# Filling, joined pieces and a state product on four quadrants in a linear-attention and two-layer kernel

## The chip, the cores and the metric

The kernel runs on one core of a Trainium2 chip. The metric is the device time of one execution in microseconds; the time before is the median of three runs. The engines are TensorE (PE; its weight loads are shown apart as PEld), VectorE (DVE), ScalarE (ACT), GpSimd (POOL) and the sync engine (SP), whose queue issues all the transfers here.

## What is computed

A gated linear attention over 4 batches, 8 heads, 768 steps and 48 features a head, and two feed-forward layers on its output. All numbers are float32.

```python
for t in range(S):                       # S = 768
    state = alpha[:, :, t, :, None] * state + einsum('bhd,bhe->bhde', k[:, :, t], v[:, :, t])
    y[:, :, t] = einsum('bhd,bhde->bhe', q[:, :, t], state)
x = y.transpose(0, 2, 1, 3).reshape(B * S, H * D)      # 3072 x 384
h = x @ w_in                                           # 384 x 2048
x = where(h > 0, h, exp(minimum(h, 0)) - 1) @ w_out
g = x @ w_gate                                         # 384 x 1536
return (g * sigmoid(g) * (x @ w_val)) @ w_out2
```

## The kernel before

**Tiling.** The 768 steps are cut into 6 chunks of 128; a unit u is one chunk of one batch (24 units, chunk c = u // 4, batch b = u % 4). In a unit the 8 heads are 4 pairs: head 2p lies on partitions 0 to 47 and head 2p+1 on 64 to 111 (`PR` = 112), the pairs side by side. The first layer works on 4 units at once (512 columns), its 384 input features in 3 blocks of 128 partitions. The heads of pairs 0 to 2 fill 96 partitions of each block; those of pair 3 are cut in three and laid into the gaps (partitions 48 to 63 and 112 to 127) by transfers.

**One unit.** `A`, `N`, `M` make the decays and scale K and Q on VectorE, ScalarE and GpSimd (on VectorE alone for u < 4). `E` multiplies K and Q (`scores`) and masks them (`causal`) into the tile A; for c > 0 it first copies the batch's state `sc` into `sbd`, a block-diagonal tile, on ScalarE. `Dk` turns K (`flip`, four transposes) and copies it out (`keep`) into KT. `Gs` makes the outer product of KT and V (`outer`) and brings `sc` up to date (`state`, VectorE). `Hy` makes the output y: `values` is the product of `sbd` and Q (four matmuls of 112x112) and that of V and A (eight, on two column tiles). `high` rounds y into the layer's input x (pairs 0 to 2) and into x3 (pair 3) on ScalarE; the remainder is made by `low` on VectorE, and for u < 4 by `minus`, a matmul with the negative identity, and `rest` on ScalarE. `gaps` moves x3 into the gaps of x, six transfers a chunk.

**PSUM.** `bank` gives the one tile `aps` (for u < 4 in turn with `acc2`) to `flip`, `outer` and `values`; `pair` gives `ape`, two banks, to `scores`.

**The layers.** `moe1` and `moe2`: each product is three matmuls of rounded and remainder parts (`mm3`), so a group of a block of features is 9 matmuls of 128x128x512. `mm1` makes h, `mm2` the accumulation acc, two groups behind. Weights come packed as raw words and are unpacked by `weight` on ScalarE and VectorE from two raw buffers. `SEGMENTS` lists the order of the first layer: (chunk, first and last block, the attention chunk added before it): chunk 0 first half with attention chunk 1; chunk 1 first half; chunk 0 second half; chunk 1 second half with attention chunk 2; then chunks 2 to 5, each with the next attention chunk. The second layer follows.

**Order.** Nothing of this is issued as it is written. Every step is `plan.add`ed with its engine and a planned duration, and `Plan.run` lays out all of them as a list schedule: at each moment the ready step with the longest tail goes first; `soon` lifts a step's rank and `lag` adds a margin ahead of it. The engines' orders are then fixed by hand (`Pinned`, line 128 records every operation, so most rows have that line). Up to the first `mm1`, `run` calls `warm` ahead of each TensorE step with the planned idle time, and `warm` puts in matmuls on zeros (tile `idle`), one for each 0.22 us; `at.warm(6.8)` puts 30 ahead of all.

## Time and profile before

| | us |
|---|---|
| median of 3 runs (989.09 to 989.59) | 989.59 |
| the profiled execution | 990.69 |
| its span, first to last instruction | 988.9 |
| TensorE busy | 973.4 |
| VectorE busy | 541.0 |
| ScalarE busy | 512.7 |
| GpSimd busy | 69.3 |

All times in the rows below are microseconds from the span's start. In a timeline row stand the start, the stretch that the merged instructions cover, the engine, the line, the operation, the tile written and the tiles read, and the number of instructions; brackets give the idle time before them and what ended it. Matmuls overlap and their ends are modelled, so a matmul group is read from start to start. A float32 matmul has two records, one in the rounded format (the layers, the transposes, `minus`) has one.

### The profile page before, as it was taken

The numbers are of one execution on the slowest core, as the hardware profiler recorded it, in microseconds if no ns is written. First come the engines' busy times: TensorE is split into PE (matmuls) and PEld (weight loads), VectorE is DVE, ScalarE is ACT, GpSimd is POOL, SyncE is SP. The second block draws the span as 40 slices with busy tenths as digits, with TensorE's granted clock in tenths as the row PEclk, the third lists the DMA queues.
The fourth block names the chain that finished last, engine by engine and source line by source line (L and its number), as shares of the span: only waits on it lengthen the run. The fifth ranks groups of instructions, "written<-read, shape, count | busy, mean of one in ns | idle before, by whom it ended". The sixth has DMA issues, their size and how long they took to land.

```text
span 988.9 us, 13352 instructions
## 1 busy us (share of the span) xinstructions
PE 973.4 (98%) x5354; PEld 811.2 (82%) x5354; DVE 541.0 (55%) x840; ACT 512.7 (52%) x910; POOL 69.3 (7%) x51
## 2 busy tenths in 40 slices
PE   9899999999999999999999999999999999999997
PEld 4577788878887888888888888888888888888886
DVE  4999888667646653533677763334333334333332
ACT  3889999666776765555898542212212212212111
POOL 0122011123211310100000000000000000000000
PEclk9999999999999999999999999999999999999999
DMA  4646434333302301100434311001001001000001
GB/s 192 222 158 209 162 114 159 108 102 118 101 1 85 129 6 43 36 14 1 160 128 183 127 52 65 1 1 64 1 1 57 8 1 45 9 1 32 1 1 36
DMA packets 20662, 72.51 MB, mean 73 GB/s; under 512 B 2672, under 2 KB 5744, under 8 KB 17648
## 3 DMA queue, kind: packets, MB, share of 16 engines
q1 hardware_dynamic: 20592, 71.58, 21.2%
q8 instruction: 44, 0.72, 0.3%
q14 instruction: 26, 0.21, 0.1%
HBM read 58.20 MB, written 11.01 MB: 70 GB/s over the span
## 4 chain that ended last, share of the span: by engine, by line
PE 91%; ACT 3%; DVE 3%; DMA 2%; issue 0%; SPq 0%; ACTq 0%; DVEq 0%
PE gv L128 30%; PE acc L128 19%; PE h L128 18%; PE q L128 15%; PE aps L128 4%; PE idle L128 2%; PE ape L128 2%; DMA in<-qkva 1%; DVE in L128 1%; ACT raw L128 1%; DVE raw L128 1%; DMA raw<-w 1%; ACT e L128 1%; ACT R L128 1%; ACT x L128 0%
## 5 line engine op out<-in xcount | busy, mean ns | idle before, releaser
L128 PE MATMUL gv<-x,wt 128*128 128x512 f32 x1296 | 308.1, 391 | 0.0
L128 PEld LDWEIGHTS gv<-x,wt 128*128 128x128 f32 x1296 | 242.2, 188 | 48.0
L128 PE MATMUL h<-x,wt 128*128 128x512 f32 x864 | 215.6, 394 | 1.4 <-DMA x<-x 1.4
L128 DVE TENSOR_TENSOR s<-gv,s 128x512 f32<-128x512 f32 x144 | 99.6, 691 | 210.7 <-ACT s L128 167.3
L128 PE MATMUL acc<-g,wt 128*128 128x512 f32 x864 | 214.5, 393 | 0.2 <-DVE g L128 0.2
L128 PEld LDWEIGHTS h<-x,wt 128*128 128x128 f32 x864 | 159.7, 188 | 37.0 <-ACT r L128 1.7
L128 PEld LDWEIGHTS acc<-g,wt 128*128 128x128 f32 x864 | 160.4, 188 | 35.0 <-DVE g L128 0.6
L128 PE MATMUL q<-wt,u 128*128 128x384 f32 x864 | 163.0, 337 | 0.0
L128 PEld LDWEIGHTS q<-wt,u 128*128 128x128 f32 x864 | 153.6, 188 | 5.6
L128 ACT ACTIVATE s<-gv 128x512 f32<-128x512 f32 x72 | 43.1, 598 | 176.6 <-PE gv L128 176.6
L128 DVE SCALAR_TENSOR_TENSOR e<-e,r 128x512 f32<-128x512 f32 x96 | 68.6, 715 | 98.0 <-ACT r L128 97.9
L128 ACT ACTIVATE u<-s 128x512 fp32r<-128x512 f32 x72 | 45.4, 631 | 123.6 <-DVE s L128 123.2
L128 ACT ACTIVATE e<-h 128x512 f32<-128x512 f32 x96 | 57.1, 595 | 67.8 <-PE h L128 67.4
L128 DVE TENSOR_TENSOR g<-e,g 128x512 fp32r<-128x512 f32 x96 | 67.3, 701 | 29.8 <-ACT g L128 29.5
L128 ACT ACTIVATE g<-e 128x512 fp32r<-128x512 f32 x96 | 60.3, 628 | 28.9 <-DVE e L128 28.5
L128 DVE SCALAR_TENSOR_TENSOR raw<-raw 128x768 int32<-128x768 int32 x68 | 67.9, 1000 | 12.0 <-ACT raw L128 10.9
L128 DVE TENSOR_TENSOR u<-s,u 128x512 fp32r<-128x512 f32 x72 | 49.8, 692 | 40.6 <-ACT u L128 40.5
L128 ACT ACTIVATE e<-e 128x512 f32<-128x512 f32 x96 | 60.7, 632 | 2.9
L128 ACT ACTIVATE raw<-raw 128x768 f32<-128x768 f32 x68 | 58.9, 905 | 3.1 <-DMA raw<-w 2.9
L128 ACT ACTIVATE r<-h 128x512 f32<-128x512 f32 x96 | 55.9, 582 | 0.0
L128 POOL TENSOR_TENSOR in<-in 112x512 f32<-112x512 f32 x20 | 30.1, 1504 | 249.9 <-DVE in L128 130.7
L128 POOL TENSOR_TENSOR in<-in,R 112x512 f32<-112x512 f32 x20 | 37.0, 1849 | 79.5 <-ACT R L128 79.5
(78 smaller groups left out, 614.7 us busy)
## 6 DMA issues: line engine op xcount, KB each, us to landing
raw<-w SPq DMA_DIRECT2D x34, 768.0 KB, 4.2
in<-qkva SPq DMA_DIRECT2D x23, 1024.0 KB, 5.4
x2r<-x2d SPq DMA_DIRECT2D x18, 256.0 KB, 3.4
out<-y SPq DMA_DIRECT2D x24, 192.0 KB, 2.0
x2d<-o SPq DMA_DIRECT2D x12, 256.0 KB, 2.3
x<-x SPq DMA_DIRECT2D x36, 64.0 KB, 4.3
half<-o SPq DMA_DIRECT2D x6, 256.0 KB, 4.0
part<-half SPq DMA_DIRECT2D x6, 256.0 KB, 6.1
```

Of the source, the lines that this page charges most:

```text
L128: ins = getattr(self.engine, name)(*a, **k)
```

## The change

- Filling: the 30 matmuls ahead of all go; one filling matmul stands for 0.36 us of planned idle time in the first stretch and for 0.25 us in the later ones, in place of 0.22 us.
- Joined pieces: for u >= 4 `scores` and `flip` are one TensorE step, and so are `outer` and `values`. The output y then lies in the `ape` tile, across its two banks, and `aps` is left to `flip` and `outer`.
- The state's product reads `sc` directly, as eight 48x48 matmuls on the four 64x64 quadrants; `sbd` and its ScalarE copies go. `CROSS` says which pairs (2 and 3) have their two heads on changed sides of x, so that pair p and pair p + 2 use the four quadrants and different banks.
- Chunk 0 (`first`): a padded copy `vz` of V's heads 6 and 7, made on GpSimd, lets 12 matmuls of V and A write all 128 partitions of the three blocks; one `high`, one `minus` and one `rest` follow, and no `gaps`.
- The first layer's w_in tiles are loaded with the halves of block 2 swapped: three transfers in place of one for 8 of the 16 tiles. `gaps` of the other chunks reads x3 by the new sides.

```diff
+CROSS = (0, 0, 1, 1)
...
-                fill(start[i] - last)
+                fill(start[i] - last, last)
...
-            syn.dma_start(out=w.raw.rearrange("p a t -> p (a t)"), in_=src.bitcast(I32))
+            to, of, n = w.raw.rearrange("p a t -> p (a t)"), src.bitcast(I32), 2 * G * 128
+            if not cross:
+                syn.dma_start(out=to, in_=of)
+                return
+            m = n * CROSS.index(1)
+            syn.dma_start(out=to[:, 0:m], in_=of[:, 0:m])
+            for j in range(2):
+                syn.dma_start(
+                    out=to[64 * j:64 * j + 64, m:KD * n], in_=of[64 - 64 * j:128 - 64 * j, m:KD * n])
...
-        plan.add("SP", 0.5, load, w=[hk, lk], kb=768)
+        plan.add("SP", 1.5 if cross else 0.5, load, w=[hk, lk], kb=768)
...
-            for _ in range(int((us - 0.2) / 0.22)):
+            for _ in range(int((us - 0.2) / (0.25 if start else 0.36))):
...
-            if c:
-                def state():
-                    for j in range(2):
-                        r = slice(64 * j, 64 * j + D)
-                        act.activation(
-                            out=self.sbd[u % 2][r, :, 64 * j:64 * j + D], in_=self.sc[b][r], func=AF.Copy)
-                plan.add("ACT", 0.65, state, r=[("sc", b)], w=[("sbd", u % 2)])
...
+            turned = self.Dk(u) if u >= B else None
+            if turned:
+                key, flip, keep = turned
+                def both():
+                    scores()
+                    flip()
+                plan.add("PE", 1.65, both, r=[K, Q], w=[*keys, key], soon=SOON, lag=MARGIN)
+                plan.add("ACT", 0.48, keep, r=[key], w=["KT"])
...
+            def apart():
+                pool.tensor_copy(
+                    self.vz[:, :, :, D:64],
+                    d["v"][:, 2 * KD:H, 0:D].rearrange("p j (i e) -> p j i e", i=KD))
+            def values():
+                d["oy"] = o = bank()
+                for p in range(KD):
+                    for j in range(2):
+                        i = j ^ CROSS[p]
+                        ten.matmul(
+                            out=o[64 * j:64 * j + 64, p * C:(p + 1) * C], lhsT=d["v"][:, 2 * p + i, :],
+                            rhs=d["A"][:, i, p], start=p == 0, stop=False)
+                for p in range(KD):
+                    for j in range(2):
+                        i = j ^ CROSS[p]
+                        ten.matmul(
+                            out=o[64 * j:64 * j + 64, p * C:(p + 1) * C], lhsT=self.vz[:, i, p],
+                            rhs=d["A"][:, i, KD], start=False, stop=p == KD - 1)
+            def high():
+                if 0 not in xt:
+                    new_x(0)
+                act.activation(
+                    out=xt[0][:, 0, :, ts], in_=d["oy"][:, 0:KD * C].rearrange("p (a c) -> p a c", a=KD),
+                    func=AF.Copy)
+            def minus():
+                ten.matmul(
+                    out=d["oy"][:, 0:KD * C], lhsT=self.neg, rhs=xt[0][:, 0, :, ts],
+                    start=False, stop=True, skip_group_check=True)
...
+                o = self.pe.tile([128, 2, 512], F32, tag="ape", name="ape").rearrange("p a n -> p (a n)")
+                d["oy"] = o = o[:, 256:768]
                 cols = [slice(p * C, (p + 1) * C) for p in range(NP)]
                 for p, cs in enumerate(cols):
-                    if c:
+                    for j in range(2):
+                        i = j ^ CROSS[p]
                         ten.matmul(
-                            out=o[0:PR, cs], lhsT=self.sbd[u % 2][0:PR, p, 0:PR], rhs=d["Q"][0:PR, p],
-                            start=p == 0, stop=False,
+                            out=o[64 * j:64 * j + (D if j else 64), cs],
+                            lhsT=v[:, 2 * p + i, 0:D] if j else v[:, 2 * p + i, :],
+                            rhs=d["A"][:, i, p], start=p % 2 == 0, stop=False,
                         )
-                for p, cs in enumerate(cols):
-                    ten.matmul(
-                        out=o[0:64, cs], lhsT=v[:, 2 * p, :], rhs=d["A"][:, 0, p],
-                        start=not c and p == 0, stop=p == NP - 1,
-                    )
-                    ten.matmul(
-                        out=o[64:PR, cs], lhsT=v[:, 2 * p + 1, 0:D], rhs=d["A"][:, 1, p],
-                        start=not c and p == 0, stop=p == NP - 1,
-                    )
+                for p in range(2):
+                    for pp in (p, p + 2):
+                        for i in range(2):
+                            j = i ^ CROSS[pp]
+                            r = slice(64 * i, 64 * i + D)
+                            ten.matmul(
+                                out=o[64 * j:64 * j + D, cols[pp]], lhsT=self.sc[b][r, pp],
+                                rhs=d["Q"][r, pp], start=False, stop=p == 1,
...
+            renew = self.Gs(u)
+            if renew:
+                okey, outer, state = renew
+                def both():
+                    outer()
+                    values()
+                plan.add("PE", 2.2, both, r=["A", V, Q, "KT", ("sc", b)], w=[key, okey],
+                         soon=SOON, lag=MARGIN)
+                plan.add("DVE", 0.65, state, r=[okey, F], w=[("sc", b)])
...
-            if b == B - 1:
+            if b == B - 1 and c:
...
-        w1[g, s] = weight(plan, lambda: P.wp, "w", w1d[g, s], 2 * NG1)
+        w1[g, s] = weight(plan, lambda: P.wp, "w", w1d[g, s], 2 * NG1, not (plan.now or s))
...
-    at.warm(6.8)
```

## Rows read from the trace of the kernel before

**Rows 1.** From the page: TensorE in part 1, busy time, share, instructions.

```profile
PE 973.4 (98%) x5354; PEld 811.2 (82%) x5354; DVE 541.0 (55%) x840; ACT 512.7 (52%) x910; POOL 69.3 (7%) x51
```

**Rows 2.** The chain that ended last, 0 to 105 us: start, duration, what.

```profile
1.07 18.50 PE idle L128 x72
...
97.85 2.35 DMA x<-x
...
100.33 2.35 PE h L128 x9
```

**Rows 3.** Windows of the filling matmuls alone: stretch, length, busy (count), clock, DMA.

```profile
1.00:6.60 5.60, 5.53 (x14) 1.00 0.70 245
6.60:19.50 12.90, 12.90 (x60) 1.00 0.62 259
...
46.00:52.00 6.00, 4.92 (x22) 1.00 0.90 327
```

**Rows 4.** Timeline of all engines, 0 to 30 us.

```profile
9.85 0.69 DVE L128 SCALAR_TENSOR_TENSOR in<-N,in 112x512 f32<-112x512 f32 x1 [0.19 <-ACT N L128]
...
19.50 1.16 PE L128 MATMUL acc<-in 48*128 48x128 f32 x16
...
20.76 1.29 DVE L128 TENSOR_TENSOR A<-acc,mask 128x512 int32<-128x512 int32 x2 [7.80 <-PE acc L128]
```

**Rows 5.** Windows of all engines: stretch, length, busy time and count of each engine.

```profile
21.20:95.90 74.70, 69.61 (x606) 51.06 (x605) 72.60 (x123) 66.11 (x129) 14.57 (x10) 1.00 0.54 187
100.30:133.00 32.70, 32.67 (x156) 26.89 (x157) 26.26 (x38) 30.35 (x51) 1.61 (x2) 1.00 0.34 124
```

**Rows 6.** Timeline of all engines, 30 to 62 us.

```profile
47.69 0.64 ACT L128 ACTIVATE x<-acc 112x128 fp32r<-112x128 f32 x2
...
48.36 3.94 SPq L128 DMA_DIRECT2D x<-x  x6
...
54.01 4.37 PE L128 MATMUL h<-x,wt 128*128 128x512 f32 x18
```

**Rows 7.** Timeline of TensorE, 215 to 300 us.

```profile
220.30 1.13 PE L128 MATMUL aps<-in,sbd 112*112 112x128 f32 x8 [0.88 <-DVE T L128]
```

**Rows 8.** Timeline of TensorE, 292 to 345 us, units 16 to 19.

```profile
293.38 2.21 PE L128 MATMUL h<-x,wt 128*128 128x512 f32 x9
...
299.28 0.67 PE L128 MATMUL aps<-in,KT 128*64 128x48 f32 x16
299.88 2.33 PE L128 MATMUL h<-x,wt 128*128 128x512 f32 x9
302.05 1.04 PE L128 MATMUL aps<-in,sbd 112*112 112x128 f32 x8
303.02 1.09 PE L128 MATMUL aps<-A,in 128*64 128x128 f32 x16
304.03 2.35 PE L128 MATMUL acc<-g,wt 128*128 128x512 f32 x9
306.32 1.16 PE L128 MATMUL ape<-in 48*128 48x128 f32 x16
307.41 0.60 PE L128 MATMUL aps<-ident,in 112*128 112x112 f32 x4
307.78 2.29 PE L128 MATMUL h<-x,wt 128*128 128x512 f32 x9
310.00 0.67 PE L128 MATMUL aps<-in,KT 128*64 128x48 f32 x16
...
342.35 2.21 PE L128 MATMUL acc<-g,wt 128*128 128x512 f32 x9
344.39 0.84 PE L128 MATMUL h<-x,wt 128*128 128x512 f32 x3
```

**Rows 9.** Timeline of TensorE, 378 to 421 us, units 20 to 23.

```profile
379.07 2.20 PE L128 MATMUL acc<-g,wt 128*128 128x512 f32 x9
...
418.93 2.21 PE L128 MATMUL h<-x,wt 128*128 128x512 f32 x9
```

More of the change, by code (lines that the diff above doesn't have):

```diff
@@ L191, in __init__, with weight @@
             self.key = key
-    def weight(plan, pool, tag, src, slots):
+    def weight(plan, pool, tag, src, slots, cross=False):
         w = Box(*turn(tag, slots))
@@ L269, in __init__ @@
             self.sc = [cp.tile([128, NP, D], F32, name=f"sc{b}") for b in range(B)]
-            self.sbd = [cp.tile([128, NP, 128], F32, name=f"sbd{b}") for b in range(2)]
             self.ident = cp.tile([128, 128], F32, name="ident")
@@ L276, in __init__ @@
             self.neg = cp.tile([128, 128], F32R, name="neg")
+            self.vz = cp.tile([128, 2, KD, 64], F32, name="vz")
             self.x3 = cp.tile([128, 2, TB], F32R, name="x3")
@@ L298, in init @@
         def init(self):
+            self.z = self.cp.tile([128, 128], BF16, name="wz")
+            vec.memset(self.z, 0.0)
             vec.memset(self.zero, 0.0)
@@ L313, in init, with warm @@
             nc.gpsimd.tensor_copy(self.mask, t)
-            for t in self.sbd:
-                nc.gpsimd.memset(t, 0.0)
-        def warm(self, us):
+        def warm(self, us, start):
             if self.idle is None:
-                self.z = self.cp.tile([128, 128], BF16, name="wz")
-                vec.memset(self.z, 0.0)
                 self.idle = ph.tile([128, TB], F32, tag="h", name="idle")
-            for _ in range(int((us - 0.2) / 0.22)):
+            for _ in range(int((us - 0.2) / (0.25 if start else 0.36))):
                 ten.matmul(
@@ L471, in causal @@
                     )
-            plan.add("PE", 1.25, scores, r=[K, Q], w=keys, soon=SOON, lag=MARGIN)
+            turned = self.Dk(u) if u >= B else None
[5 more added lines that the diff above has]
+                plan.add("PE", 1.65, both, r=[K, Q], w=[*keys, key], soon=SOON, lag=MARGIN)
+                plan.add("ACT", 0.48, keep, r=[key], w=["KT"])
+            else:
+                plan.add("PE", 1.25, scores, r=[K, Q], w=keys, soon=SOON, lag=MARGIN)
             plan.add("DVE", 1.24 if len(keys) > 1 else 1.1, causal, r=keys, w=["A"])
@@ L503, in state, with first, rest @@
                 vec.tensor_tensor(out=sc[0:PR], in0=kv, in1=pc, op=ALU.mult)
+            if c:
+                return key, outer, state
             plan.add("PE", 0.75, outer, r=["KT", V], w=[key], soon=SOON, lag=MARGIN)
-            plan.add("DVE", 0.65 if c else 0.3, state, r=[key, F], w=[("sc", b)])
+            plan.add("DVE", 0.3, state, r=[key, F], w=[("sc", b)])
+        def first(self, u):
+            d, (F, K, Q, V) = self.u[u], self.keys(u)
+            key, bank = self.bank(u)
+            ts = slice(u * C, (u + 1) * C)
+            xk = ("x", 0, u)
+            def apart():
[26 more added lines that the diff above has]
+                    start=False, stop=True, skip_group_check=True)
+            def rest():
+                act.activation(
+                    out=xt[0][:, 1, :, ts], in_=d["oy"][:, 0:KD * C].rearrange("p (a c) -> p a c", a=KD),
+                    func=AF.Copy)
+            plan.add("POOL", 0.4, apart, r=[V], w=["vz"], port=True)
+            plan.add("PE", 1.5, values, r=["A", V, "vz"], w=[key], soon=SOON, lag=MARGIN)
+            plan.add("ACT", 0.45, high, r=[key], w=[xk])
+            plan.add("PE", 0.25, minus, r=[xk], w=[key], soon=SOON)
+            plan.add("ACT", 0.45, rest, r=[key], w=[xk])
@@ L508, in Hy @@
         def Hy(self, u):
+            if u < B:
+                self.first(u)
+                return
             d, (F, K, Q, V) = self.u[u], self.keys(u)
             c, b = divmod(u, B)
-            key, bank = self.bank(u)
             ts = slice(b * C, (b + 1) * C)
-            xk, gk = ("x", c % 2, b), ("x3", b)
+            xk, gk, key = ("x", c % 2, b), ("x3", b), ("ape",)
             def values():
                 v = d["v"]
-                d["oy"] = o = bank()
+                o = self.pe.tile([128, 2, 512], F32, tag="ape", name="ape").rearrange("p a n -> p (a n)")
+                d["oy"] = o = o[:, 256:768]
@@ L610, in step @@
                 self.N(u + 1)
-            self.Gs(u)
+            if u < B:
+                self.Gs(u)
             if nxt:
@@ L619, in step @@
                 self.load(u + INS)
-            if nxt:
+            if nxt and u + 1 < B:
                 self.Dk(u + 1)
```

32 lines of the change are left out of this document (11 added, 21 removed).

## Prediction

> **What bounds the kernel now.** I read first the page's busy table: TensorE is busy 98% of the span [rows 1], so time is saved only by taking work off TensorE or out of a stretch where its busy time is not work. Then the chain that ended last: its first long piece is 72 filling matmuls on zeros, 1.07 to 19.57 us, counted as busy [rows 2]. They are no work. By the windows of the filling alone, the first 14 took 5.53/14 = 0.40 us each and the next 58 to 60 0.215 us each [rows 3]: that is 512 columns at the lower of TensorE's two levels (1.2 GHz), then at the upper (2.4), though the granted clock reads 1.00 for both. The planner had counted 0.22 us for each. What did the first real matmul need? K of unit 0 was finished by VectorE at 9.85 + 0.69 = 10.54 us; the scores started at 19.50, and VectorE stood idle for 7.80 us until it could mask them at 20.76 [rows 4]. From there to the end of chunk 1 VectorE is busy 72.60 of 74.70 us [rows 5]: it, not TensorE, paces that part. At 100.33 the second segment's first product starts, behind a transfer of the layer's input that lands late [rows 2]. After that TensorE is the bound: 32.67 of the next 32.70 us [rows 5].
>
> So there are three stages: start to 100.33 us, paced by filling and VectorE; the first layer with attention units 8 to 23 between its products, paced by TensorE; the second layer, untouched by the change.
>
> **The start.** 30 filling matmuls before the initial work go, and the first stretch is divided by 0.36 instead of 0.22. The planned start was such that 42 fitted: (t - 0.2)/0.22 = 42 to 43, t = 9.44 to 9.66, and so 25 or 26 now. At the prices of rows 3 they take 14 x 0.40 + 11 x 0.215 = 8.0 us and end near 9.1, ahead of K. Scores(0) then start near 10.7, are done near 11.8, and VectorE, busy with unit 1 until 20.76 - 7.80 = 12.96, finds them ready. Its whole 7.80 us gap closes, and all that it paces moves 7.8 us forward.
>
> Next late is the input of the first layer. Unit 3's remainder is written at 47.69 + 0.64 = 48.33; six transfers are issued on SP's queue over 3.94 us from 48.36; 22 filling matmuls hold TensorE meanwhile [rows 3]; and the first product starts at 54.01 [rows 6]. The change builds chunk 0's columns whole in PSUM (heads 6 and 7 laid into the gaps by a padded copy of V), so those six transfers and this filling's place go. It pays 12 V products a unit against 8 (0.5 us more of TensorE, by the 1.01 us of eight [rows 8]) and a small GpSimd copy a unit; of two ScalarE copies and two subtracting matmuls one each is left. TensorE has filling to give up there, so I cost the products at nothing; uncovered they are 4 x 0.5 = 2 us. GpSimd's copy is queued alone there; uncovered it delays each unit's V product by less than 0.5 us. The first product can begin near 48.3 - 7.8 = 40.5.
>
> But it does not follow that the segment ends 13.5 us earlier: VectorE's work to the end of chunk 1 is unchanged. It offers 7.8 us plus its idle 74.70 - 72.60 = 2.1. I take 10 us for the start of the second segment, 100.33. TensorE's own bound is looser: 54.01 to 100.33 is 46.3 us, less 1.3 of waiting, from 40.5 gives 85.5, a gain of 14.8, the upper end. For the lower end I take 5: eight weights are loaded by three transfers instead of one, on the SP queue in front of the next loads of inputs and weights; an issue cost 3.94/6 = 0.66 us [rows 6], so 1.3 us more a weight for a queue that otherwise waits for buffers. Four such delays on the path would take 5.2 of the 10.
>
> **TensorE between the products.** All costs are read from start to start, since the ends are modelled. A nine-matmul group costs 344.39 - 342.35 = 2.04 us. A unit's pieces: scores 1.09 (306.32 to 307.41), transposes of K 0.37 behind them, outer product 0.60, state product 0.97 (302.05 to 303.02), V product 1.01. A group behind a piece takes about 0.13 more (299.88 to 302.05 is 2.17), one in front of an outer product or scores 0.09 more (307.78 to 310.00: 2.22, so only 0.09 behind transposes) [rows 8].
> What units cost in all: from 293.38 to 342.35 are four units and 15 groups: (48.97 - 30.60)/4 = 4.59 each [rows 8]. The last chunk, without transposes and outer products, from 379.07 to 418.93 with 13 groups: (39.86 - 26.52)/4 = 3.34 [rows 9].
>
> After: scores and transposes in one piece, 0.09 + 1.09 + 0.37 + 0.09 = 1.64; outer, V and state product in one piece, 0.09 + 0.60 + 1.01 + s + 0.14 = 1.84 + s; together 3.48 + s. The last chunk: 1.32 + 1.21 + s = 2.53 + s, the scores no longer directly behind a V product, since both now use one PSUM tile.
> The price s of eight 48x48x128 products on the four quadrants isn't in the trace. Nearest rows: the outer product, eight small products on two tiles, 0.60; below it, half of 1.01, 0.51, if two rounds run at the V product's pair price; above, 1.02, no better than the V product's two tiles. I take 0.59, the outer product's, since it has as many instructions and narrow weights. Then a unit saves 4.59 - 4.07 = 0.52 and in the last chunk 3.34 - 3.12 = 0.22: 12 x 0.52 + 4 x 0.22 = 7.1. One wait of 0.88 for the state's sum also goes, since the products no longer need the outer product's bank [rows 7]. Gain: 8.0. In general it is 17.5 - 16 s.
> The Trainium skill (TensorE: Matmul & The Clock Gate, Part 3, Measured speedup vs the span model) says that a pack of tiles lasts as long as one matmul plus some 4 ns a tile; estimated by it s would be about 0.51 and the total 1.3 us lower, and no row here shows four tiles at once.
>
> ScalarE loses 40 state copies and waits less; it is off the path after 100 us, so nothing. New waits: scores(u+1) wait for ScalarE's and VectorE's reading of y(u), and a joined piece waits for the later of its inputs (K turned and the masked scores), with all of the layer's products queued behind it on TensorE. Two groups between the pieces, 4.1 us, cover each; where the plan leaves fewer, the price is a wait of the size of the 0.88 us one [rows 7], at most once a unit or 14 us, which I take as unlikely and leave to A's end of the range.
>
> **Sum.** 10 + 8 = 18 us. The profiled execution took 990.69 with a span of 988.9; the median of the runs is 989.59. From the median: 971.6.
>
> **Rivals.**
> (A) The quadrants run only two at a time, or the array empties at each change of shape. s = 1.02 gives 17.5 - 16.3 = 1.2, total 978.4. For it: no row shows quadrants. Against: scores on two row tiles are followed by full-array transposes with no added time (1.09 either way) [rows 8].
> The Trainium skill (TensorEngine Tiling (Array Packing), Key Properties) says "Mode switching requires drain"; one 0.16 us emptying on each side of the state product would give 16 x 0.32 = 5 us back.
> (B) The start gives only 5: weights come late through the threefold loads, or thinner filling lets TensorE fall to its lower level, doubling pieces of 1 us on the path of four units. Total 976.6. Against: filling pieces remain between the units.
> (C) Slower: the four quadrants run one after another at a full product's price, 0.97/4 = 0.24 each: s = 1.94, a loss of 13.5 against the start's 10, total 993.1. It decides from 17.5 - 16 s = -10, s = 1.72 (0.215 a product). Against: both kinds of two-tile products cost 0.13 each.
> (D) The filling doesn't give way: another operand holds scores(0) at 19.5. Then only the 8.0 is left: 981.6. Against: the idle VectorE of rows 4.
>
> **How the numbers follow.** Forecast 0.63, A 0.15, B 0.11, C 0.04, D 0.04, something within 2 us of now 0.03. The forecast alone spans 966 (14.8 and s = 0.51) to 975. The range takes in A and B: 965 to 981. Faster by over 0.2% (2 us, about what a measurement of this kernel tells from no change) 0.93, within 0.03, slower 0.04.
>
> **What would show it.** In the profile after: about 25 filling matmuls before scores(0), scores(0) near 10.7 us, no long VectorE gap; the first h product near 41; the second segment near 90, not 100; eight state products (16 records) within about 0.6 us; units at 4.1 us; the second layer's 448 us unchanged. A first product that moves forward while the second segment doesn't would prove the start's step wrong; units at 4.6, the quadrants'.

## The result and the profile after

| | median us | runs | ratio to before, 95% interval |
|---|---|---|---|
| before | 989.59 | 989.09 to 991.75 | 1 |
| after | 979.48 | 978.03 to 981.59 | 0.9898 [0.9882, 0.9914] |

The kernel is faster by 10.1 us, not by the 18 that were forecast. The profiled execution of after took 978.03 us with a span of 976.2. It is the lowest of its four runs; that of before, 990.69, lies 1.1 above the median that the prediction started from. So the two profiles lie 12.7 us apart and the medians 10.1, and 2.6 us of what the stretches below gain are a matter of which executions were profiled. Two borders divide both spans: the second segment's first product (the ninth group of nine h products) and the first product of the second layer, which in before is this row of TensorE's timeline (start, duration, what):

```profile
533.55 2.66 PE L128 MATMUL gv<-x,wt 128*128 128x512 f32 x11
```

| stretch | before us | after us | gained | predicted |
|---|---|---|---|---|
| start to the second segment | 100.33 [rows 2] | 96.76 | 3.6 | 10 |
| from there to the second layer | 433.22 | 423.81 | 9.4 | 8.0 |
| second layer to the end | 455.35 | 455.63 | -0.3 | 0 |

So the shortfall is all in the start. Four views of after show it. First the page, TensorE's line of part 1 and the granted clock of part 2:

```profile
PE 952.7 (98%) x5471; PEld 796.0 (82%) x5471; DVE 546.3 (56%) x840; ACT 497.4 (51%) x862; POOL 73.1 (7%) x54
...
PEclk9989999999999999999999999999999999999999
```

TensorE still fills 98%, with 20.7 us less than in [rows 1], but the clock line is no longer a row of nines: its third slice, about 49 to 73 us, has an 8. TensorE's timeline of after, in the start and at both borders (in brackets the idle time before it and who ended it):

```profile
1.07 7.92 PE L128 MATMUL idle<-wz 128*128 128x512 bf16 x29 [1.07 <-DVE zero L128]
...
12.24 1.16 PE L128 MATMUL acc<-in 48*128 48x128 f32 x16
...
37.80 1.14 PE L128 MATMUL acc<-A,in 128*64 128x128 f32 x12 [2.34 <-ACT KT L128]
...
42.22 4.85 PE L128 MATMUL h<-x,wt 128*128 128x512 f32 x18
...
48.47 2.30 PE L128 MATMUL h<-x,wt 128*128 128x512 f32 x9
...
55.58 2.08 PE L128 MATMUL ape<-in 48*128 48x128 f32 x16 [2.75 <-DVE x L128]
...
58.28 4.11 PE L128 MATMUL acc<-g,wt 128*128 128x512 f32 x9
...
96.76 2.32 PE L128 MATMUL h<-x,wt 128*128 128x512 f32 x9 [2.00 <-DMA x<-x]
...
520.57 3.79 PE L128 MATMUL gv<-x,wt 128*128 128x512 f32 x16
```

The filling is shorter, the scores of unit 0 stand at 12.24 instead of 19.50 [rows 4], and the first product of the layer at 42.22 instead of 54.01 [rows 6]: 11.8 us earlier. Eight groups of h later only 3.6 of that are left. Behind the first product two long waits show on TensorE: 2.75 us ahead of the scores of unit 5, which need the PSUM tile that VectorE is still reading y of unit 4 from, and 2.00 ahead of the second segment, behind the transfers of chunk 1's gaps. What follows the first wait runs at half pace: scores 2.08 instead of 1.16, nine products 4.11 where such a group behind a piece took 2.35 in [rows 8]. (The first product has a smaller one of the kind ahead of it: after the wait of 2.34 us at 37.80 the granted clock read 0.61 up to 42.20, and the first 18 products took 4.85 instead of 4.37 [rows 6].) The windows of all engines (stretch, length, busy time of PE, PEld, DVE, ACT, POOL, granted clock, DMA share, GB/s):

```profile
12.90:95.00 82.10, 71.49 (x660) 53.57 (x656) 76.20 (x124) 63.15 (x113) 22.35 (x14) 0.94 0.55 184
...
56.00:58.30 2.30, 2.30 (x21) 2.08 (x19) 1.56 (x3) 1.28 (x3) 0.00 (x0) 0.50 0.86 345
58.30:62.30 4.00, 4.00 (x11) 2.76 (x9) 4.00 (x6) 3.36 (x7) 0.00 (x0) 0.52 0.10 41
```

The granted clock reads 0.50 and 0.52 in that place, the lower of TensorE's levels. VectorE is busy for 76.20 us of the 82.10 after its first scores; before it was 72.60 of 74.70 [rows 5]. The chain that ended last, 0 to 110 us, says what this cost:

```profile
54.66 0.68 DVE x L128 x2
55.58 2.08 PE ape L128 x16
...
89.43 7.25 DMA x<-x
```

It runs through VectorE's reading of y, the wait and the slow products, then through VectorE, and comes to the second segment by the transfers x<-x: 7.25 us for 64 KB each. In before the same step stands with 2.35 [rows 2]. The queue of SP (start of the issue, duration, what) shows what lies in front of them:

```profile
84.10 2.36 SPq L128 DMA_DIRECT2D raw<-w  x4
86.68 0.40 SPq L128 DMA_DIRECT2D in<-qkva  x1
87.35 4.33 SPq L128 DMA_DIRECT2D x<-x  x6
```

Four transfers of two weight tiles and 1 MB of unit 10's input go out in the 3.2 us before the six. They land 5.9 to 8.2 us after their issue (median 7.4).

The second gain is plain in the timeline of TensorE, units 16 to 18, the place of [rows 8]; one unit of after:

```profile
297.97 1.16 PE L128 MATMUL ape<-in 48*128 48x128 f32 x16
...
299.44 2.30 PE L128 MATMUL acc<-g,wt 128*128 128x512 f32 x9
301.67 0.61 PE L128 MATMUL aps<-in,KT 128*64 128x48 f32 x15
302.07 0.30 PE L128 MATMUL ape<-A,in 128*48 128x128 f32 x1
...
302.17 1.05 PE L128 MATMUL ape<-A,in 128*64 128x128 f32 x15
303.15 0.65 PE L128 MATMUL ape<-in,sc 48*48 48x128 f32 x16
303.74 2.34 PE L128 MATMUL h<-x,wt 128*128 128x512 f32 x9
```

One piece of scores and transposes, one of outer product, V product and state product (the V products' first record is at 302.07, among the last of the outer product). The state product lasts from 303.15 to 303.74: 0.59 us, where [rows 8] has 0.97.

### The profile page after: what moved, and what is told of

It is laid out like the page before. It is cut to its first block, busy times and chain, and to the rows that moved or that the text cites. A ratio compares the mean times of both kernels' runs of the same rounds, so it can differ in the third digit from the quotient of the medians.

```text
span 976.2 us, 13567 instructions
## 1 busy us (share of the span) xinstructions
PE 952.7 (98%) x5471; PEld 796.0 (82%) x5471; DVE 546.3 (56%) x840; ACT 497.4 (51%) x862; POOL 73.1 (7%) x54
## 4 chain that ended last, share of the span: by engine, by line
PE 91%; DVE 3%; DMA 3%; ACT 1%; issue 1%; SPq 1%; DVEq 0%; ACTq 0%
PE gv L128 30%; PE acc L128 20%; PE h L128 19%; PE q L128 16%; PE ape L128 5%; PE aps L128 2%; DMA raw<-w 1%; DMA x<-x 1%; DVE in L128 1%; DMA in<-qkva 1%; DVE raw L128 1%; SPq L128 1%; DVE A L128 0%; DVE wt L128 0%; DVE e L128 0%
## 5 line engine op out<-in xcount | busy, mean ns | idle before, releaser
L128 DVE SCALAR_TENSOR_TENSOR raw<-raw 128x768 int32<-128x768 int32 x68 | 66.5, 984 | 11.3 <-ACT raw L128 10.4
L128 DVE TENSOR_TENSOR u<-s,u 128x512 fp32r<-128x512 f32 x72 | 49.8, 692 | 40.6 <-ACT u L128 40.5
L128 ACT ACTIVATE raw<-raw 128x768 f32<-128x768 f32 (+1 forms) x68 | 59.0, 905 | 3.5 <-DMA raw<-w 2.9
L128 POOL TENSOR_TENSOR in<-in 112x512 f32<-112x512 f32 x20 | 35.7, 1787 | 207.7 <-DVE in L128 153.4
L128 ACT ACTIVATE R<-R 112x512 f32<-112x512 f32 x48 | 30.2, 630 | 23.1 <-DVE R L128 22.6
```

Of the source, the lines that this page charges most:

```text
L128: ins = getattr(self.engine, name)(*a, **k)
```

## The experiments

Twelve runs, each against the kernel before on the same chip. The table puts together what their timelines of TensorE show, in us: the first work that is no filling (scores or transposes of unit 0), the first product of layer 1, the start of the second segment, the stretch from there to the second layer, and the median with its range. All but the last column are read from one execution, which can lie off the median (e12's was 2.5 us above it, e8's 2.5 below), and the first product differs by 2.6 us among executions that begin with the same work (after, e3, e4, e5, e9).

| kernel | first work | first product | second segment | stretch | median (range) |
|---|---|---|---|---|---|
| before | 19.50 | 54.01 | 100.33 | 433.2 | 989.59 (989.09 to 991.75) |
| after | 11.69 | 42.22 | 96.76 | 423.8 | 979.48 (978.03 to 981.59) |
| e1_fill_only | 10.67 | 45.89 | 93.01 | 431.8 | 981.43 (980.73 to 982.21) |
| e2_old_fill | 20.4 | 49.73 | 107.24 | 425.2 | 989.41 (985.46 to 990.92) |
| e3_y4_apart | 12.2 | 43.74 | 98.00 | 426.1 | 980.64 (979.83 to 981.17) |
| e4_gaps_first | 11.7 | 42.58 | 94.96 | 431.0 | 983.67 (982.59 to 985.63) |
| e5_filled_wait | 12.4 | 44.84 | 98.26 | 423.9 | 978.72 (975.50 to 982.38) |
| e7_apart | 11.9 | 47.28 | 94.36 | 432.8 | 984.94 (982.73 to 987.51) |
| e8_one_load | 11.7 | 41.07 | 96.40 | 423.6 | 979.31 (976.82 to 980.04) |
| e9_in10_later | 11.6 | 43.45 | 97.54 | 425.4 | 979.21 (977.33 to 980.35) |
| e10_chunk0_old | 10.4 | 51.23 | 97.75 | 425.1 | 979.25 (977.78 to 979.82) |
| e12_first2_old | 10.0 | 50.30 | 103.89 | 425.3 | 983.78 (982.48 to 986.31) |
| e13_first2_old_one | 10.0 | 45.96 | 92.56 | 424.7 | 974.97 (973.65 to 976.11) |
| e14_one_replan | 11.9 | 41.10 | 92.82 | 424.8 | 975.20 (974.47 to 977.34) |

### Which part does what: the filling alone, and all but the filling

e1: the kernel before with the new filling only.

```diff
-    at.warm(6.8)
...
-            for _ in range(int((us - 0.2) / 0.22)):
+            for _ in range(int((us - 0.2) / (0.25 if start else 0.36))):
```

> The kernel before with the new filling alone (no 30 matmuls ahead, 0.36 and 0.25 us for one). Theory (VectorE paces the start, so its closed gap of 7.8 us comes out at the second segment): scores(0) near 10.7 us, second segment near 92.5 in place of 100.33, time near 982. Rival (whatever the start gains, transfers, weights and new waits of TensorE give back before the second segment): scores(0) near 10.7, but the second segment at 96 or later, time 985 to 988.

e2: the changed kernel with the old filling.

```diff
+    at.warm(6.8, 0)
     at.init()
...
-            for _ in range(int((us - 0.2) / (0.25 if start else 0.36))):
+            for _ in range(int((us - 0.2) / 0.22)):
```

> The changed kernel with the old filling (30 matmuls ahead, 0.22 us for one); the plan's order is the same. Theory (filling is most of the start's gain): scores(0) near 19.5, first product some 8 us later than 42.2, second segment near 102, time 984 to 987. Rival (other parts bind the start, and more filling keeps TensorE at its upper level): first product later, second segment still near 97 to 98, no fall of the clock near 55 us, time within 1 us of 979.5.

Measured: e1 0.9913 [0.9899, 0.9927], e2 0.9986 [0.9974, 0.9998]. The window of all engines over VectorE's part in e1:

```profile
13.00:95.00 82.00, 72.87 (x618) 54.32 (x617) 80.14 (x133) 71.94 (x140) 16.86 (x11) 1.00 0.57 192
```

The filling by itself brings the second segment from 100.33 to 93.01, 7.3 us, and VectorE is busy 80.14 of 82.00: no idle time left but what it had. That is the 7.80 us gap of [rows 4], moved to the end, and no more. All the other edits without the filling (e2) shorten the stretch behind the second segment by 8.0 us and lengthen the start by 6.9: next to nothing comes of them, less than either expectation had. So the change does not add up: 7.3 from the filling and some 8 to 9 from the products would be 16, and 10 came. Something in the other edits costs the start what they gain later.

### Is it the wait of 2.75 us, and the clock after it?

e3: y of unit 4 goes to two banks of the layer's accumulators, free at that time, so that scores(5) need not wait; the order of all work is left as it was.

```diff
             def values():
                 v = d["v"]
+                if u == B:
+                    o2 = [pacc.tile([128, 512], F32, tag=f"acc{j}", name=f"acc{j}") for j in range(2)]
+                    d["oy"] = o2
+                    self.products(u, lambda a, b, cs: o2[cs.start // 256][a:b, cs.start % 256:cs.start % 256 + C])
+                    return
                 o = self.pe.tile(
```

> The changed kernel with y of unit 4 in two free accumulation banks instead of the tile that unit 5's scores need; the plan's order is the same; one more small copy on ScalarE and VectorE for that unit. Theory (the shared tile held TensorE for 2.75 us at 52.8 and the clock fell after it): scores(5) at 52.9 at 1.1 us, the accumulation that ended at 62.32 ends near 59.5, and the second segment comes up to 3 us earlier if the transfers allow it. Rival (VectorE paces this stretch): TensorE then waits for VectorE's g near 57 instead, the clock falls as before, and the second segment stays within 1 us of 96.8.

e5: twelve filling matmuls in the place of the wait.

```diff
                 def both():
+                    if u == B + 1:
+                        o = pacc.tile([128, 512], F32, tag="acc0", name="idle2")
+                        for _ in range(12):
+                            ten.matmul(
...
                     scores()
                     flip()
```

> The changed kernel with 12 filling matmuls (2.6 us) ahead of unit 5's joined scores, where TensorE waited 2.75 us and came back at its lower level; nothing else moves. Theory (TensorE's pace sets the second segment): scores(5) at 1.1 us in place of 2.0, the accumulation behind it 2.2 in place of 4.0, TensorE some 3 us earlier at 62 us, second segment up to 2 us earlier. Rival (VectorE's chain and the gap transfers set it): TensorE is warm, but the second segment stays at 96 to 97.5 and the time at 979.5 within 1 us.

Measured: e3 0.9903 [0.9888, 0.9917], e5 0.9883 [0.9863, 0.9904]. TensorE in e3, then in e5:

```profile
54.28 1.16 PE L128 MATMUL ape<-in 48*128 48x128 f32 x16
...
57.06 0.47 PE L128 MATMUL acc<-g,wt 128*128 128x512 f32 x1 [1.09 <-DVE x L128]
58.54 3.35 PE L128 MATMUL acc<-g,wt 128*128 128x512 f32 x8 [1.00 <-DVE g L128]
```

```profile
59.80 1.16 PE L128 MATMUL ape<-in 48*128 48x128 f32 x16
...
61.26 2.29 PE L128 MATMUL acc<-g,wt 128*128 128x512 f32 x9
```

And the gap transfers of chunk 1 on SP's queue, again in e3 and e5:

```profile
87.11 5.06 SPq L128 DMA_DIRECT2D x<-x  x6
```

```profile
89.32 3.94 SPq L128 DMA_DIRECT2D x<-x  x6
```

In e3 the scores run at 54.28 without a wait, and TensorE stands 1.09 and 1.00 us before the next group instead, for VectorE's x and g; the slow products come there (3.35 for eight). In e5 nothing is slow there, nine products take 2.29, and the second segment still begins at 98.26, behind a wait of 1.53 for x<-x. The profiled execution of e5 had its first product 2.6 us later than that of after (the scores of unit 0 ran at half pace in it, 2.08 instead of 1.16, and ScalarE waited for weights, of which more below), so 98.26 alone would prove little; the medians, 979.48 without the filling and 978.72 with it, show no difference either. But the wait isn't free. From the third group of h (48.47 in after, 49.99 in e3, 52.68 in e5) to the issue of the gap transfers it is 38.9 us in after, 37.1 in e3 and 36.6 in e5; of this VectorE is idle for 2.60, 1.04 and 0.52. In e4, e8 and e9, which keep the wait, it is 38.9 to 39.0 again. So the wait, with the slow products behind it, holds up the way to the gap transfers by some 2 us. In e5 the later beginning took this back, in e3 the later beginning and a slower landing (8.9 us for 64 KB). What it is worth in time, these medians can't tell.

### Is it the queue in front of the gap transfers?

e4: the same work, with the load of unit 10 and that of the ninth weight tile put behind the six gap transfers. e9: with unit 10's load alone put behind them.

```diff
+        for tag in ("w8", "in10"):
+            i = self.tags[tag]
+            if order.index(i) < order.index(self.tags["gaps1"]):
+                order.remove(i)
+                order.insert(order.index(self.tags["gaps1"]) + 1, i)
         for i in order:
```

> The changed kernel with the six gap transfers of chunk 1 issued ahead of the loads of unit 10 and of the ninth weight tile; nothing else moves. Theory (the 7.25 us of these transfers are queueing behind those loads): they land in 2 to 4 us, TensorE's wait of 2.00 us at the second segment goes, it starts near 94.8, time 977.5. Rival (the transfers are slow by themselves or the two loads, now later, are needed): landing stays above 6 us, or another wait of some 2 us appears within the next 30 us.

> The changed kernel with the gap transfers of chunk 1 ahead of the 1 MB load of unit 10 alone; the ninth weight tile keeps its place, so ScalarE doesn't wait for it. Theory (the transfers queue behind loads, and the loss in the run that moved both came from the weight tile): they land in 4 to 6 us in place of 7.4, the second segment starts at 94.8 to 95.5, ScalarE has no wait for a weight over 2 us, time near 978. Rival (unit 10's load is needed as well): another wait of 2 us appears.

Measured: e4 0.9939 [0.9926, 0.9952], e9 0.9884 [0.9868, 0.9900]. With both loads moved the gap transfers land in 2.4 us (median), as in before; with unit 10's alone in 4.7. So the 7.4 of after is the queue. In neither does TensorE wait for them. But e4 pays for it. TensorE, then ScalarE (L135 is the line that records every operation in this kernel):

```profile
101.91 0.80 PE L135 MATMUL acc<-g,wt 128*128 128x512 f32 x1 [4.75 <-ACT g L135]
102.99 3.69 PE L135 MATMUL acc<-g,wt 128*128 128x512 f32 x8 [0.28 <-DVE g L135]
```

```profile
99.68 0.88 ACT L135 ACTIVATE raw<-raw 128x768 f32<-128x768 f32 x1 [6.96 <-DMA raw<-w]
```

The weight tile is late: ScalarE waits 6.96 us for it and TensorE 4.75 for ScalarE's g, and the next eight products take 3.69 us. e9 has no such wait, and its second segment is no earlier: its first product came at 43.45, and the first 18 products took 6.46 us instead of 4.85. The place of unit 10's load alone is not worth anything that these runs could tell.

### Is it the new way to write chunk 0?

e10: units 0 to 3 write their output as before (part to x3, six gap transfers), on the new sides.

```diff
-            if u < B:
-                self.first(u)
-                return
...
-            if b == B - 1 and c:
+            if b == B - 1:
                 self.gaps(c)
```

> The changed kernel with chunk 0's output made as before (four pairs, pair 3 through x3 and six gap transfers); filling, joined pieces, quadrants and changed sides stay. Theory (VectorE's chain to the end of chunk 1 sets the second segment, so an earlier first product is worth nothing): first product 3 to 5 us later than 42.2, second segment within 1.5 us of 96.8 or earlier, time 976 to 981. Rival (chunk 0's direct output is worth what it saves): second segment 3 us or more later, time 982.5 or more.

Measured: 0.9886 [0.9870, 0.9902]. One row of TensorE:

```profile
51.23 7.17 PE L128 MATMUL h<-x,wt 128*128 128x512 f32 x18 [3.22 <-DMA x<-x]
```

The first product comes 9.0 us later than in after, behind the gap transfers, and the second segment at 97.75, 1.0 later; the time is the same. The early first product, the most visible gain of after, is worth nothing: the segment waits for units 4 to 7 and their transfers, whenever it began. (e13 below, whose first product comes 4.9 us later than e14's, is as fast as e14.)

### What is the joining worth?

e7: four pieces a unit instead of two, everything else as changed, planned anew.

```diff
-                plan.add("PE", 1.65, both, r=[K, Q], w=[*keys, key], soon=SOON, lag=MARGIN)
+                plan.add("PE", 1.25, scores, r=[K, Q], w=keys, soon=SOON, lag=MARGIN)
+                plan.add("PE", 0.45, flip, r=[K], w=[key], soon=SOON, lag=MARGIN)
...
-                plan.add("PE", 2.2, both, r=["A", V, Q, "KT", ("sc", b)], w=[key, okey],
-                         soon=SOON, lag=MARGIN)
+                plan.add("PE", 0.75, outer, r=["KT", V], w=[okey], soon=SOON, lag=MARGIN)
+                plan.add("PE", 1.7, values, r=["A", V, Q, ("sc", b)], w=[key],
+                         soon=SOON, lag=MARGIN)
```

> The changed kernel with scores and transposes, and outer product and values, as four steps of the plan instead of two joined ones; the plan lays out a new order. Theory: in chunks 2 to 5 a unit costs 0.3 to 0.5 us more at the edges of its pieces, some 4 to 6 us in all from the second segment to the second layer, the state product still 0.59. Rival (the edges were cheap, since pieces stood together anyway): the same stretch within 2 us of the changed kernel's 423.8.

Measured: 0.9950 [0.9933, 0.9967]; the stretch behind the second segment is 432.8, as long as in before, and 9.0 longer than in after. The median is only 5.5 above that of after, since the second segment begins 2.4 earlier with less work done: 14 outer products and 13 sets of transposes lie behind it, 12 of each in after, some 2 us by the prices below. TensorE at two places:

```profile
134.08 0.66 PE L128 MATMUL ape<-in,sc 48*48 48x128 f32 x16
134.67 0.67 PE L128 MATMUL aps<-in,KT 128*64 128x48 f32 x16
...
274.89 0.55 PE L128 MATMUL aps<-ident,in 112*128 112x112 f32 x4
275.21 2.33 PE L128 MATMUL acc<-g,wt 128*128 128x512 f32 x9
277.37 2.21 PE L128 MATMUL h<-x,wt 128*128 128x512 f32 x9
```

The state product takes 134.67 - 134.08 = 0.59 here too. But the transposes stand alone between groups: 0.32 for themselves and 2.16 instead of 2.04 for the group behind (275.21 to 277.37), 0.44 in place of the 0.37 that they cost behind the scores (299.07 to 299.44 in after). The outer product does the same (0.59 and 0.14 behind it at 279.51, against 0.40 to 0.50 within a joined piece), and three waits of TensorE (0.87, 0.56 and 0.46) are in the stretch, which after doesn't have. So the quadrants without the joining, in this plan, keep 0.4 us of the 9.4 that the stretch gained, or some 2.5 with the moved work allowed for: most of what the cheaper pieces save is paid back at the borders between pieces and in waits. How much of it is borders and how much the other plan was not separated.

### Is it the weights in three transfers?

Eight of the first layer's weight tiles, those that meet the input with changed sides, are loaded by three transfers each (the expectation of e8 says nine). With the features permuted once where the inputs are laid out, before the launch, one does. e8: this alone, in the order of after. e12: chunks 0 and 1 worked as before (own pieces, the widened state product, the one-bank output), chunks 2 to 5 as changed, three transfers. e13: as e12 with one transfer. e14: after with one transfer. The last three are planned anew, with the transfer's own length on SP (1.5 for three, 0.5 for one). The edit of e14 (e8 has the second part of it, and loads each tile by one transfer while the plan still counts 1.5):

```diff
-        w1[g, s] = weight(plan, lambda: P.wp, "w", w1d[g, s], 2 * NG1, not (plan.now or s))
+        w1[g, s] = weight(plan, lambda: P.wp, "w", w1d[g, s], 2 * NG1)
...
-            r[i, j, :D] = (2 * i + j) * D + np.arange(D)
-            r[i, j, D:] = (2 * KD + j) * D + i * GAP + np.arange(GAP)
+            h = j ^ CROSS[i]
+            r[i, j, :D] = (2 * i + h) * D + np.arange(D)
+            r[i, j, D:] = (2 * KD + h) * D + i * GAP + np.arange(GAP)
```

Of the lines by which e12 differs from after (it has those of e10, and others that give chunk 1 its widened state back), these set the joining:

```diff
-            turned = self.Dk(u) if u >= B else None
+            turned = self.Dk(u) if u >= 2 * B else None
...
-            if c:
+            if c > 1:
                 return key, outer, state
```

> The changed kernel with one edit: the layer's input is permuted where the inputs are laid out before the launch, so that the nine first-layer weight tiles of the crossed kind come in one transfer each instead of three, with the order of all work left as it was. Rival (the three transfers for a tile, and the longer queue that they make ahead of the chunk-1 gap transfers, are what holds the second segment at 97): the gap transfers land in about 3.6 to 4.7 us, as with the filling alone, the second segment begins at 93 to 95 and the median is 976 to 977. Theory (the tile's bytes are the same, and the second segment is held by VectorE's and TensorE's work of units 4 to 7): second segment at 96 to 98, landing 6 to 8 us, median 979 to 980.

> The changed kernel with chunks 0 and 1 worked as in the kernel before (own pieces for scores, transposes, outer product and output, the widened state product, output in the one-bank tile), only with the heads on their new sides; chunks 2 to 5 and the filling as changed; planned anew. Theory (the start loses what the filling gave through the new shape of units 4 to 7): second segment at 93 to 94 as with the filling alone, the stretch from there to the second layer at 424 as in the changed kernel, span 93.5 + 424 + 455.5 = 973, median 974 to 976. Rival (the start is slower for another reason, the weight tiles in three transfers each): second segment at 97, median 979 to 980. Second rival (the stretch is short only because the start is long, work being moved across the border between them): second segment 93, stretch 428 to 431, median 979 to 981.

> The kernel with chunks 0 and 1 worked as before and the rest as changed, and with the layer's input permuted before the launch so that every weight tile comes in one transfer; planned anew. Theory: as with the weight tiles in three transfers, second segment at 93 to 94, median 974 to 976. Rival (the three transfers a tile hold the start): 93 to 94 and 974 to 976 here, but 97 and 979 to 980 with three transfers. Second rival (work moved across the border): 979 to 981 in both.

> The changed kernel with the layer's input permuted before the launch, so that every weight tile comes in one transfer, and planned anew with the shorter occupation of SP that a single transfer has. It completes a square: new or old shape of chunks 0 and 1, weight tiles in three transfers or in one, each planned for itself; three corners stand at a second segment of 96.8 (new, three), 103.9 (old, three) and 92.6 (old, one). Theory (the three transfers cost the start, directly and through the plan that has to find room on SP for them; the shape of units 4 to 7 is innocent): second segment at 92 to 94, stretch near 424, median 973.5 to 975.5. Rival (both are needed: the new shape of units 4 to 7, whose work VectorE paces, holds the second segment by itself): second segment at 96 to 98, median 978.5 to 980.

Measured: e8 0.9903 [0.9888, 0.9918], e12 0.9940 [0.9926, 0.9954], e13 0.9859 [0.9843, 0.9874], e14 0.9858 [0.9838, 0.9877]. TensorE in e8, e12, e13 and e14, in this order:

```profile
96.40 2.32 PE L128 MATMUL h<-x,wt 128*128 128x512 f32 x9 [2.74 <-DMA x<-x]
```

```profile
103.89 3.79 PE L128 MATMUL h<-x,wt 128*128 128x512 f32 x9 [6.17 <-DMA x<-x]
```

```profile
92.56 2.37 PE L128 MATMUL h<-x,wt 128*128 128x512 f32 x9 [1.41 <-DMA x<-x]
```

```profile
54.47 2.08 PE L128 MATMUL ape<-in 48*128 48x128 f32 x16 [2.75 <-DVE x L128]
...
92.82 2.20 PE L128 MATMUL h<-x,wt 128*128 128x512 f32 x9
...
96.14 2.11 PE L128 MATMUL acc<-g,wt 128*128 128x512 f32 x8 [0.57 <-DVE g L128]
```

My theory for e12, that the new shape of units 4 to 7 costs the start, is wrong: with the old shape and three transfers the second segment comes at 103.89, the latest but e2's. With one transfer it comes at 92.56 (old shape) and 92.82 (new shape). So with one transfer the shape makes no difference, and the three transfers, with the plan that is made for them, cost the start 11.3 us in the one shape and 3.9 in the other. In time, which the spread of single executions touches less, that is 983.78 - 974.97 = 8.8 and 979.48 - 975.20 = 4.3. It is the rival of e13 (with e12 later than it said) and the theory of e14 that came true. The queue of SP in e14, to be read beside that of after:

```profile
82.87 1.20 SPq L128 DMA_DIRECT2D raw<-w  x2
85.39 4.13 SPq L128 DMA_DIRECT2D x<-x  x6
89.69 0.45 SPq L128 DMA_DIRECT2D in<-qkva  x1
```

The same two tiles in two transfers, then the gap transfers, two us earlier than in after (85.39 against 87.35), and unit 10's load behind them. They land in 4.8, and TensorE goes into the second segment without a wait.

The 3.9 us from after to e14 can be followed: the first product 1.1 earlier (41.10 against 42.22); from scores(5) to the border 0.8 less without the wait there (54.47 to 92.82, 38.35, against 55.58 to 96.76 less 2.00, 39.18); and that wait of 2.00 gone. The first of these is seen on ScalarE, the first row from after, the second from e14:

```profile
14.93 2.63 ACT L128 ACTIVATE raw<-raw 128x768 f32<-128x768 f32 x3 [0.64 <-DMA raw<-w]
17.45 0.70 ACT L128 ACTIVATE N<-N,bias 112x512 f32<-112x512 f32 x1
```

```profile
14.40 2.49 ACT L128 ACTIVATE raw<-raw 128x768 f32<-128x768 f32 x3
16.78 0.72 ACT L128 ACTIVATE N<-N,bias 112x512 f32<-112x512 f32 x1
```

In after ScalarE waits for the first weight tile that comes in three, and N of the next unit is queued behind that weight on ScalarE: 17.45 against 16.78. A second such wait, 1.05 us, follows at 29.90; all five executions that begin like after have two (0.6 to 1.6 and 1.1 to 2.9 us), e8 and e14 have none. (In e5 the second is 2.9 us, and its first product the latest of all with this beginning.) In e8 and e14 the first product stands at 41.07 and 41.10; in the five runs that begin with the same work and three transfers (after, e3, e4, e5, e9) at 42.22 to 44.84. The wait of 2.75 ahead of scores(5) is there in both. e8 shows that the transfers themselves, in an unchanged order, bring only this first part (its second segment still waits 2.74 us, and the median did not move). e8 and e14 do the same work with the same transfers and differ in the order alone: 979.31 against 975.20. So most of the loss comes through the plan, which counts 1.5 us of SP for a tile of the crossed kind and puts the work of all engines in another order for it. Which part of that order matters is open: unit 10's load behind the gap transfers is one (it is all that e9 moves), and does not do it alone. Nor was the reverse run, three transfers planned as one.

What holds e14's start now? Two windows of all engines:

```profile
12.90:91.00 78.10, 68.78 (x656) 51.57 (x653) 73.04 (x123) 62.27 (x112) 20.90 (x14) 0.93 0.52 181
62.00:93.00 31.00, 30.02 (x258) 24.03 (x255) 29.34 (x50) 24.41 (x44) 10.09 (x5) 1.00 0.61 199
```

From 62 us to the border TensorE is busy 30.02 of 31.00 us and VectorE 29.34, so neither has much to spare; VectorE has 5.06 us of idle time since its first scores, most of it before. The chain that ended last runs through the wait of 2.75 us ahead of scores(5) and the slow products behind it, stays with TensorE to 63.42, and then goes through VectorE and ScalarE alone, past the border, to 96.14, where TensorE waits 0.57 us for VectorE's g. So the late transfers are off the path and that wait is on it. Whether e14 gains by filling it was not run.

e13 and e14 are faster than both kernels: 975 us, their intervals wholly below that of after.

## Why the prediction was half right

**The state product, 0.59: right to the hundredth.** It lies at 303.15 to 303.74 in the unit above, and at 0.58 and 0.59 in the other units. So the outer product's 0.60 was the right row to take, and rivals A (1.02) and C (1.94) fell. The Trainium skill (TensorE: Matmul & The Clock Gate, Part 3, Measured speedup vs the span model) let me estimate 0.51; the trace is above it. What the Trainium skill says in TensorEngine Tiling (Array Packing), Key Properties, that a change of tiling mode drains the array, cannot be seen as added time here: the V product in two tiles in front of the quadrants takes 1.01 to 1.02 (four places in the last chunk, such as 374.37 to 375.39; above its first product runs among the outer product's last), against 1.01 where a full-array group follows [rows 8].

**The steady part, 8.0: it was 9.4, and its working was a little too dear.** Units of after, start to start from 291.76 to 344.40, are three with 20 groups of 2.04: (52.64 - 40.80)/3 = 3.95, against the 4.07 of the sum and 4.59 before. The joined outer product costs 0.40 to 0.50 (301.67 to 302.07 or 302.17) and not 0.60, its first products running into the next. The last chunk, 366.84 to 407.99 with 14 groups, gives (41.15 - 28.56)/4 = 3.15 against 3.12. Then 12 x 0.64 + 4 x 0.19 + the wait of 0.88 that went, which doesn't come again in this stretch, is 9.3. But e7 corrects what I put this down to: the joining was in the sum only by its 0.09 and 0.13 for a border, and taking it away cost 5.5 us of the median.

**The new waits, taken as unlikely: they came,** for the shared tile once, with 2.75 us, and for K turned by a joined piece with up to 0.71, in the start only. I had argued that two groups between the pieces, 4.1 us, would cover it; at scores(5) the plan left none. By the traces of e3 and e5 it holds up VectorE and the gap transfers by some 2 us, which I had put at nothing in the sum.

**The start, 10: the step that failed.** Its parts, with what they measured:
- The gap of VectorE closes by 7.8: right. e1, e13 and e14 bring the second segment 7.3, 7.8 and 7.5 us forward. The scores of unit 0 stand at 12.24, after TensorE's transposes at 11.69, a little later than the 10.7 of the sum, since VectorE finishes K of unit 0 at 11.59 and not at 10.54; 29 filling matmuls stand before them, not 25. The GpSimd copies, put at under 0.5 us, took 0.27 to 0.78.
- VectorE's 2.1 us of idle time between are to be had too: wrong. No run got more than 7.8. In after VectorE has 5.9 us of idle time, more than before, waiting for TensorE's products (1.4 and 1.1) and ScalarE (1.0): I took all idle time of the engine that paces for slack; some of it is a link of the chain. Some 2 us of it came with the new wait for the shared tile.
- The first product near 40.5: right with 42.22, and worth nothing (e10).
- Eight weights by three transfers: priced at 1.3 us of SP a weight, up to 5.2 in all, and put into the lower end and into rival B. It belonged into the sum. The issue took nearly what I said (2.36 us for a tile in three and a tile in one at 84.10, against 1.20 for two in one in e8). But it isn't through four late weights that it acts. It makes ScalarE wait for the first tile and the first product 1.1 later, it keeps SP's queue taken, and the plan that knows this sets the gap transfers of chunk 1 behind 1 MB of input as well as two weight tiles, where they take 7.4 us, not the 4.8 of e14. All together 3.9 us, and by e8 the greater part through the plan. The 2.5 us left of the 6.4 that the start fell short are what e14 still misses, with the wait for the shared tile in it; how much of them that wait is, no run shows.

So rival B was what happened, by the first of its two reasons: I gave it 5 us of gain at the start and 976.6 in all; it came to 3.6. Its second reason, the lower clock level, happened too; together with the wait ahead of it, it cost the some 2 us that e3 and e5 show.

That 979.48 lies inside the stated range is owed to the range, which took in A and B, and not to the sum: the forecast alone reached to 975, and a steady part 1.4 better than forecast hid part of what the start lost.

From 971.6 to 979.48 the terms are: start 6.4, steady part -1.4, second layer 0.3, and 2.6 because the profiled execution of before was 1.1 above its median and that of after 1.4 below.

## What to carry to other kernels

Closing an engine's idle gap is worth the gap of the engine that paces the stretch, here 7.3 to 7.8 us of 7.80; a first product that comes 11.8 us earlier adds nothing to it. A tile that two pieces share makes a new wait, and a wait that no median shows can still lie on the path: compare the same piece of the chain in executions with and without it. Before a load is cut into three, count what stands behind it in its queue: it cost 4 to 9 us here, most of it in the one pair that tells it apart through the planner's price for the longer issue, and data permuted before the launch cost none of it. A small piece of work between large ones costs at its borders too, so joining pieces (5.5 us here) can be worth as much as making one of them cheaper, and only a run with one of the two undone shows it.

## What the runs showed of the hardware

- Eight 48x48x128 products on four quadrants take 0.58 to 0.59 us, where four products of 112x112x128 on the whole array take 0.97 [rows 8], and going from two tiles to quadrants adds nothing that the rows show.
- After a wait of TensorE of 2.75 us the granted clock read 0.50 and 0.52 from 56.0 to 62.3 us; after waits of 4.75 (e4) and 3.22 (e10) the next products ran slow too (3.69 for eight, 7.17 for 18). After 2.34 us in after it read 0.61 from 37.8 to 42.2 us. The same beginning did not always end alike: after 2.69 us of idle time at 9 to 11.69 us in after the scores took the usual 1.16, after 3.08 in e3 and 3.01 in e5 they took 2.08, with 0.50 from 12.4 to 18.0 us in e5.
- A transfer of 64 KB lands in 2.4 us, in 4.7 behind two weight tiles of 768 KB (e9), or in 7.4 behind these and 1 MB of input that were issued within 3.3 us before (e4 against after).
